# Linear attention twice, gated: loading the first x tile in halves, and one denominator pass per query block

## The chip, the cores and the metric

The kernel runs on one core of one Trainium2 chip. Its time is the device time of one execution in microseconds; lower is better. The time before is the median of 4 runs.

## The reference

Two linear attention blocks A and B read the same x (2048 x 640, bf16) with weights of their own; a gate mixes them.

```python
# x: [1, 2048, 640]; H = 32 heads of 20
qkv = (x @ wqkv).reshape(B, S, 3, H, Dh) ...        # q, k, v
phi = lambda t: jnp.where(t > 0, t + 1, jnp.exp(t)) + 1e-6
pq, pk = phi(q), phi(k)
kv  = jnp.einsum("bhsd,bhse->bhde", pk, v)
z   = jnp.einsum("bhsd->bhd", pk)
num = jnp.einsum("bhqd,bhde->bhqe", pq, kv)
den = jnp.einsum("bhqd,bhd->bhq", pq, z)[..., None] + 1e-6
block = (num / den) ... @ wo
# with g = sigmoid(sum(x * gate_w)):
out = g * A_block + (1 - g) * B_block
```

## The kernel before, in words

**Names.** XN is x by rows (16 tiles of 128 rows), XT its transpose. WK, WQ, WV, WO are the weights of A and B; a weight's "chunk" c is 128 of its 640 rows. PK and PQ are the features phi(k) and phi(q); they share one buffer, FEA for A and FEB for B, so the profile calls both FEA or FEB. ps is PSUM, 8 banks of 512 float columns.

**Stages.** First, keys: x tiles 0 to 3 are loaded by rows and transposed on TensorE (`transpose_x`, L480), and DVE copies the transposes from PSUM to XT (L488); tiles 4 to 15 come transposed by DMA. `k_part` multiplies a tile by WK in 5 chunks; `phi_k` makes the features with one ACT exponential (L506) and two DVE instructions (L510, L515). Second, `g_unit` multiplies the key features by x, which gives the sums from which `m_unit` (a product with WV and a mask into MB on DVE, L607) and `wp_unit` (a product of MB with WO, copied to WS) build one matrix WP per attention block; WP goes through DRAM (`wrows`) by `wp_rows`. The sums of the key features end up in ZBD. Third, queries: `q_unit` makes 512 columns of query features for one of 5 feature groups: 5 matmuls of 512 columns, an exponential on ACT into one of 6 EK slots (L699), and two DVE instructions (L703, L708) that end in PQ. Ten units (5 of A, 5 of B) make a block of 512 rows; there are 4 blocks. Then `dens` multiplies PQ by ZBD, 4 narrow column groups side by side (two for A, two for B), and `scale_q` adds eps (L743), takes the reciprocal (L749), sends it through DRAM to be spread over heads (`factor`, RX), and multiplies PQ by it in place (L767). Last, `final` multiplies PQ of a tile of 128 rows by WP, for A and for B, and mixes both with the gate (ACT L815, DVE L821) before the output DMA.

**Order.** All operations are listed in the program with the keys they read and write. A planner (`_Sched.schedule`) fixes at build time the order of each engine, with estimated durations: it gives each engine the operation that can start first, and among those within 20 ns the one that comes first in the program. PSUM banks, EK slots and the like are handed out in the same walk. On the chip every engine then runs its list in order and waits on semaphores. The operations of the first key tiles are chained (`after=at[0]`), so TensorE does them in program order:

```python
warm(7)
transpose_x(0)
warm(1)
transpose_x(1)
first("A", (0, 0), (0, 1))          # (tile, chunk)
warm(1)
first("A", (1, 0), (1, 1))
first("A", (0, 2), (1, 2), (0, 3), (1, 3))
transpose_x(2)
```

`warm` is a matmul of 512 columns on constants. DMAs are issued from SP's and from ACT's queue; all matmuls but the transposes are recorded at L395, all DMAs at L384.

Of the kernel before, what the change touches and what calls it, by code (L numbers as in the profile page):

```python
# [19 lines left out]
D = 640  # L20
# [4 lines left out]
NC = 5  # L25
EPS = 1e-6
HALF = 320
XW = 672
PE_GHZ = 2.4

# [276 lines left out]
def _dve_ns(n, rate=1):  # L307
    return n / (0.96 * rate) + 68.0
# [6 lines left out]
def bass_gated_mix__linear_attn_block__linear_attn_block__prompt_kernel(nc, A_x, A_wqkv, A_wo, B_x, B_wqkv, B_wo, gate_w, out):  # L315
# [6 lines left out]
    with ExitStack() as es:  # L322
# [89 lines left out]
            ),  # L412
            400, writes=[("ID",)], name="id1",
        )
        for X in XS:
            sch.op("POOL", lambda e, X=X: e.memset(WO[X][:, 5, :], 0.0), 500, writes=[("WO5", X)], name="woz" + X)
        sch.op("POOL", lambda e: e.memset(MB[:, 5, :], 0.0), 200, writes=[("M", 5)], name="mz")
        def load_x(eng, t):
            dma(eng, "xn%d" % t, XN[:, t, 0:D], xin[128 * t : 128 * t + 128, :], writes=[("XN", t)], us=0.25)

        def load_wk(eng, c):
            dma(eng, "wkA%d" % c, WK["A"][:, c, :], weights("A", D, c, c + 1)[:, 0, :], writes=[("WK", "A", c)], us=0.25)

        load_wk("ACT", 0)
        load_x("SP", 0)
        load_wk("ACT", 1)
        load_x("SP", 1)
        load_wk("ACT", 2)
        load_wk("SP", 3)
        load_wk("ACT", 4)  # L430
        load_x("SP", 2)
        load_x("ACT", 3)
        for c0, c1 in ((0, 1), (1, 3), (3, 5)):
            dma(
                "SP", "wkB%d" % c0, WK["B"][:, c0:c1, :], weights("B", D, c0, c1), writes=[("WK", "B", c) for c in range(c0, c1)],
# [38 lines left out]
        def transpose_x(t):  # L474
            tt = _Tile(1)

            def fn(pe):
                ins = None
                for c in range(NC):
                    ins = pe.transpose(PSB[:, tt.banks[0], 128 * c : 128 * c + 128], XN[:, t, 128 * c : 128 * c + 128], IDN[:, :])  # L480
                return ins

            at[0] = sch.op(
                "PE", fn, 5 * 112, reads=[("XN", t), ("ID",)], writes=[(tt,)], name="xpose%d" % t, lat=190, after=at[0]
            )
            sch.op(
                "DVE",
                lambda e: e.tensor_copy(  # L488
                    XT[:, :, 128 * t : 128 * t + 128], PSB[:, tt.banks[0], 0:D].rearrange("p (c f) -> p c f", f=128)
                ),  # L490
                _dve_ns(D), reads=[(tt,)], writes=[("XT", t)], name="xev%d" % t,
            )

        ring = {"ek": _Ring(NEK), "dn": _Ring(2), "rx": _Ring(2), "os": _Ring(NOS), "ts": _Ring(NTS)}

# [26 lines left out]
        def k_part(X, t, tile, cs, chain=False):  # L522
            xc = slice(128 * t, 128 * t + 128)
            order = [(h, c) for h in (0, 1) for c in cs] if len(cs) == NC else [(h, c) for c in cs for h in (0, 1)]

            def steps():
                return [
                    (PS[:, tile.banks[h], 0:HALF], XT[:, c, xc], WK[X][:, c, HALF * h : HALF * h + HALF], c == 0, c == NC - 1, None)
                    for h, c in order
                ]  # L530

            o = mms(
                "k%s%d_%d" % (X, t, cs[0]), steps, [("XT", t)] + [("WK", X, c) for c in cs], [(tile,)], len(cs) * (D + 12),
                after=at[0] if chain else None,
            )
            if chain:
                at[0] = o
# [81 lines left out]

        def wp_unit(X, q):  # L620
            tile = _Tile(2)
            n = 120

            def steps():
                return [
                    (PS[0:n, tile.banks[h], 0:HALF], MB[0:n, q, 0:n], WO[X][0:n, q, HALF * h : HALF * h + HALF], True, True, None)
                    for h in (0, 1)
                ]

            mms("wp%s%d" % (X, q), steps, [("M", q), ("WO", X), ("WO5", X)], [(tile,)], D + 60)  # L630
            dst = WS[0:n, q, :].rearrange("p (h f) -> p h f", f=HALF)

            def src():
                return PS[0:n, tile.banks[0] : tile.banks[1] + 1, 0:HALF]

            name = "wpe%s%d" % (X, q)
            if X == "A" and q % 2 == 0:
                sch.op("DVE", lambda e: e.tensor_copy(dst, src()), _dve_ns(D), reads=[(tile,)], writes=[("WS", q)], name=name)
            else:
                sch.op("ACT", lambda e: e.activation(dst, src(), ACT.Copy), _act_ns(D), reads=[(tile,)], writes=[("WS", q)], name=name)  # L640
# [39 lines left out]
        def q_unit(X, b, k):  # L680
            tile = _Tile(1)
            es = _Tile(1, ring["ek"])

            def ek():
                return EK[:, es.slot, 0:512]

            dst = PQ[X][:, k, 512 * b : 512 * b + 512]
            span = range(S * k + 512 * b, S * k + 512 * b + 512)
            over = [("F", X, "k", t) for t in range(span[0] // D, span[-1] // D + 1)]

            def steps():
                return [
                    (PS[:, tile.banks[0], :], WQ[X][:, c, k : D : NC], XT[:, c, 512 * b : 512 * b + 512], c == 0, c == NC - 1, None)
                    for c in range(NC)
                ]

            mms("q%s%d%d" % (X, b, k), steps, [("XT", t) for t in range(4 * b, 4 * b + 4)] + [("WQ", X)], [(tile,)], NC * 518, after=gone[X])
            sch.op(
                "ACT", lambda e: e.activation(ek(), PS[:, tile.banks[0], :], ACT.Exp), _act_ns(512), reads=[(tile,)],  # L699
                writes=[(es,)], name="eq%s%d%d" % (X, b, k),  # L700
            )
            sch.op(
                "DVE", lambda e: e.tensor_scalar(ek(), ek(), 1.0, EPS, op0=ALU.min, op1=ALU.add), _dve_ns(512, 4),  # L703
                reads=[(es,)], writes=[(es,)], name="tq%s%d%d" % (X, b, k),
            )
            sch.op(
                "DVE",
                lambda e: e.scalar_tensor_tensor(  # L708
                    out=dst, in0=PS[:, tile.banks[0], :], scalar=0.0, in1=ek(), op0=ALU.max, op1=ALU.add
                ),  # L710
                _dve_ns(512), reads=[(tile,), (es,)], writes=[("PQ", X, k, b)] + over, name="sq%s%d%d" % (X, b, k),
            )

        def dens(b0):

            dtile = _Tile(1)

            def den():
                r = []
                for k in range(NC):  # L720
                    for x, X in enumerate(XS):
                        q = PQ[X][:, k, 512 * b0 : 512 * b0 + 1024].rearrange("p (b h f) -> p b h f", b=2, h=2)
                        for h in (0, 1):
                            g = 2 * x + h
                            r.append((
                                PS[32 * g : 32 * g + 32, dtile.banks[0], :].rearrange("p (b f) -> p b f", b=2), ZBD[X][:, k, :],
                                q[:, :, h, :], k == 0, k == NC - 1, (0, 32 * g),
                            ))
                return r

            mms(
                "den%d" % b0, den, [("ZBD", X) for X in XS] + [("PQ", X, k, b) for X in XS for k in range(NC) for b in (b0, b0 + 1)],
                [(dtile,)], 5 * 540,
            )
            return dtile

        def scale_q(b, dtile, pieces):

            ds = _Tile(1, ring["dn"])
            lo = 256 * (b % 2)  # L740
            sch.op(
                "DVE",
                lambda e: e.tensor_scalar(DN[:, ds.slot, :], PS[:, dtile.banks[0], lo : lo + 256], EPS, None, op0=ALU.add), _dve_ns(256),  # L743
                reads=[(dtile,)], writes=[(ds,)], name="dn%d" % b,
            )

# [135 lines left out]
            wp_unit("A", q)  # L882
        wp_rows("A")
        zbd("B")
        def queries(b):
            for X in XS:
                for k in range(NC):
                    q_unit(X, b, k)
                    if b == 1 and X == "A":
                        wp_unit("B", k)  # L890

        def finals(b):
            for t in range(4 * b, 4 * b + 4):
                if t < NT - 1:
                    final(t)
                else:
                    final(t, ((0, 320), (320, 480), (480, D)), {320: 0, D: 320})

        queries(0)
        m_unit("B", 0)  # L900
        m_unit("B", 1)
        queries(1)
        wp_unit("B", 5)
        wp_rows("B")
        d01 = dens(0)
        scale_q(0, d01, 2)
        queries(2)
        queries(3)
        scale_q(1, d01, 2)
        d23 = dens(2)  # L910
        finals(0)
        scale_q(2, d23, 2)
        finals(1)
        scale_q(3, d23, 4)
        finals(2)
        finals(3)

        sch.schedule()
        sch.plan()
# [31 lines left out]
```

## Time and profile before

| | |
|---|---|
| median of 4 runs | 193.91 us (193.54 to 195.27) |
| profiled execution | 195.42 us, span 193.6 us, 1.82 us around it |
| PE busy | 187.7 us, 97% of the span |
| DVE busy | 129.6 us, 67% |
| ACT busy | 73.6 us, 38% |
| granted TensorE clock | 1.00 in the whole span |
| keys | PE from 4.9 us |
| queries | PE from 97.8 to 146.0 us |
| finals | PE from 146.0 to 191.0 us |

The span runs from the first to the last instruction of the profiled execution. Busy time is the time in which an engine has an instruction running; idle time counts only where the engine that sets the end is idle. Rows give engine, line of the source, operation, and what is written from what. A matmul row lasts longer than its place in the stream, since matmuls overlap; the distance between the starts of two rows is what one of them costs.

### The profile page before, as it was taken

The numbers are of one execution on the slowest core, as the hardware profiler recorded it, in microseconds if no ns is written. First come the engines' busy times: TensorE is split into PE (matmuls) and PEld (weight loads), VectorE is DVE, ScalarE is ACT, GpSimd is POOL, SyncE is SP. The second block draws the span as 40 slices with busy tenths as digits, with TensorE's granted clock in tenths as the row PEclk, the third lists the DMA queues.
The fourth block names the chain that finished last, engine by engine and source line by source line (L and its number), as shares of the span: only waits on it lengthen the run. The fifth ranks groups of instructions, "written<-read, shape, count | busy, mean of one in ns | idle before, by whom it ended". The sixth has DMA issues, their size and how long they took to land.

```text
span 193.6 us, 3194 instructions
## 1 busy us (share of the span) xinstructions
PE 187.7 (97%) x1318; PEld 133.1 (69%) x1323; DVE 129.6 (67%) x249; ACT 73.6 (38%) x112; POOL 2.7 (1%) x12
## 2 busy tenths in 40 slices
PE   8699999999999999999999999999999999999994
PEld 3477777777788888888865655555556677777773
DVE  1188888888800008995169977899999997943323
ACT  2055455454411111203265477645654223332232
POOL 5000000000000000000000000000000000000000
PEclk9999999999999999999999999999999999999999
DMA  6989799996012311121145402353300135411112
GB/s 179 310 164 204 139 389 253 295 245 172 7 28 40 37 34 34 34 37 34 34 89 133 156 0 64 109 176 115 97 0 3 36 128 153 141 65 40 68 68 68
DMA packets 30609, 21.17 MB, mean 109 GB/s; under 512 B 15492, under 2 KB 30340, under 8 KB 30596
## 3 DMA queue, kind: packets, MB, share of 16 engines
q1 hardware_dynamic: 29876, 20.16, 40.8%
q10 hardware_dynamic: 720, 0.82, 1.3%
q8 instruction: 10, 0.16, 0.4%
q14 instruction: 3, 0.02, 0.0%
HBM read 12.06 MB, written 5.31 MB: 90 GB/s over the span
## 4 chain that ended last, share of the span: by engine, by line
PE 93%; DMA 3%; DVE 1%; ACT 1%; ACTq 0%; issue 0%
PE ps L395 92%; DMA WKA<-in_A_wqkv_dram 3%; DVE MB L607 1%; ACTq L384 0%; DVE FEB L708 0%; ACT EK L699 0%; PE ps L480 0%; ACT TS L815 0%; DVE OL L821 0%; DVE EK L703 0%
## 5 line engine op out<-in xcount | busy, mean ns | idle before, releaser
L506 ACT ACTIVATE EK<-ps 128x640 bf16<-128x640 f32 x32 | 22.4, 703 | 25.0 <-PE ps L395 25.0
L699 ACT ACTIVATE EK<-ps 128x512 bf16<-128x512 f32 x40 | 23.9, 597 | 20.1 <-PE ps L395 19.6
L815 ACT ACTIVATE TS<-ps,GA 128x640 f32<-128x640 f32 (+2 forms) x18 | 13.2, 734 | 31.0 <-PE ps L395 31.0
L395 PE MATMUL ps<-WPB,FEB 128*128 128x320 bf16 (+1 forms) x165 | 24.7, 295 | 0.0
L395 PE MATMUL ps<-WPA,FEA 128*128 128x320 bf16 (+1 forms) x165 | 24.7, 295 | 0.0
L395 PE MATMUL ps<-WKA,XT 128*128 128x320 bf16 x160 | 23.1, 299 | 1.6 <-DMA WKA<-in_A_wqkv_dram 1.6
L395 PE MATMUL ps<-XT,WQA 128*128 128x512 bf16 x96 | 22.6, 379 | 0.2
L395 PE MATMUL ps<-XN,FEB 128*128 128x320 bf16 (+1 forms) x160 | 22.5, 300 | 0.0
L395 PE MATMUL ps<-WKB,XT 128*128 128x320 bf16 x160 | 22.4, 299 | 0.0
L395 PE MATMUL ps<-XT,WQB 128*128 128x512 bf16 x99 | 22.2, 379 | 0.1
L395 PE MATMUL ps<-XN,FEA 128*128 128x320 bf16 (+1 forms) x160 | 22.0, 300 | 0.0
L821 DVE SCALAR_TENSOR_TENSOR OS<-ps,GA,TS 128x640 bf16<-128x640 f32 x15 | 13.0, 874 | 12.8 <-PE ps L395 11.4
L557 ACT ACTIVATE GS<-ps 128x640 bf16<-128x640 f32 x10 | 7.0, 703 | 37.1 <-PE ps L395 37.1
L395 PEld LDWEIGHTS ps<-XN,FEA 128*128 128x128 bf16 x160 | 18.8, 117 | 3.0
L395 PEld LDWEIGHTS ps<-WKA,XT 128*128 128x128 bf16 x160 | 15.4, 98 | 7.9 <-DMA WKA<-in_A_wqkv_dram 1.9
L395 PEld LDWEIGHTS ps<-XN,FEB 128*128 128x128 bf16 x160 | 18.7, 118 | 2.9
L395 PEld LDWEIGHTS ps<-WPA,FEA 128*128 128x128 bf16 x165 | 15.9, 98 | 6.1
L395 PEld LDWEIGHTS ps<-WPB,FEB 128*128 128x128 bf16 x165 | 15.8, 98 | 6.2 <-issue 0.4
L395 PEld LDWEIGHTS ps<-WKB,XT 128*128 128x128 bf16 x160 | 15.7, 98 | 6.1
L395 PEld LDWEIGHTS ps<-XT,WQB 128*128 128x128 bf16 x100 | 11.7, 117 | 9.7
L395 PEld LDWEIGHTS ps<-XT,WQA 128*128 128x128 bf16 x100 | 11.6, 118 | 8.8 <-issue 0.4
L661 DVE SCALAR_TENSOR_TENSOR GP<-XN,GWB 128x640 bf16<-128x640 bf16 x16 | 13.3, 833 | 4.1 <-PE ps L395 3.6
(52 smaller groups left out, 151.2 us busy)
## 6 DMA issues: line engine op xcount, KB each, us to landing
out_dram<-OS SPq DMA_DIRECT2D x15, 160.0 KB, 1.8
XN<-in_A_x_dram SPq DMA_DIRECT2D x3, 640.0 KB, 8.4
factor<-RC SPq DMA_DIRECT2D x4, 256.0 KB, 2.6
RX<-factor SPq DMA_DIRECT2D x4, 256.0 KB, 2.7
WVA<-in_A_wqkv_dram SPq DMA_DIRECT2D x1, 800.0 KB, 12.4
WQA<-in_A_wqkv_dram SPq DMA_DIRECT2D x1, 800.0 KB, 15.5
WVB<-in_B_wqkv_dram SPq DMA_DIRECT2D x1, 800.0 KB, 16.9
WQB<-in_B_wqkv_dram SPq DMA_DIRECT2D x1, 800.0 KB, 16.5
```

Source lines behind the costliest of these rows:

```text
L395: ins = pe.matmul(o, l, r, start=a, stop=z, tile_position=tp, skip_group_check=True)
L506: "ACT", lambda e: e.activation(ek2(), pair(tile, HALF), ACT.Exp),
L557: "ACT", lambda e: e.activation(GS[:, k, :].rearrange("p (h f) -> p h f", f=HALF), pair(tile, HALF), ACT.Copy),
L607: return e.tensor_tensor(out=MB[0:n, qq[0] : qq[-1] + 1, 0:n].rearrange("p q (i k) -> p q k i", k=NC), in0=PS[0:n, tile.banks[0], at : at ...
L661: lambda e, t=t: e.scalar_tensor_tensor(out=GP[:, :], in0=XN[:, t, 0:D], scalar=1.0, in1=GWB[:, :], op0=ALU.mult, op1=ALU.mult, accum_out= ...
L699: "ACT", lambda e: e.activation(ek(), PS[:, tile.banks[0], :], ACT.Exp), _act_ns(512), reads=[(tile,)],
L815: "ACT", lambda e, acc=acc, t_ap=t_ap: e.activation(t_ap(), acc(), ACT.Copy, scale=GA[:, 0, t : t + 1]),
L821: lambda e, acc=acc, t_ap=t_ap, o_ap=o_ap: e.scalar_tensor_tensor(out=o_ap(), in0=acc(), scalar=GA[:, 1, t : t + 1], in1=t_ap(), op0=ALU.m ...
```

## The change

- The first x tile is loaded as two column halves, one on SP's queue and one on ACT's, both ahead of the WK chunks, and the chunks and the next x tiles are dealt anew over the two queues.
- The DVE copies of the transposes of tiles 0 and 1 go in two pieces (chunks 0 and 1, then 2 to 4), and a key product waits for the piece with its chunk alone.
- Three memsets on POOL are gone; the product for WP's last group of 40 rows uses 40 rows instead of 120 rows with zeros.
- Denominators: one pass per query block with 256 columns a matmul, 4 passes, where there was one per two blocks with 512 columns, 2 passes.
- The order at the end: each block's factor follows its queries, and the finals of block b - 2 follow the queries of block b.

```diff
--- before.py
+++ after.py
@@ -25,6 +25,7 @@
 NC = 5
 EPS = 1e-6
 HALF = 320
+AHEAD = 2
 XW = 672
 PE_GHZ = 2.4
 
@@ -412,24 +413,25 @@
             ),
             400, writes=[("ID",)], name="id1",
         )
-        for X in XS:
-            sch.op("POOL", lambda e, X=X: e.memset(WO[X][:, 5, :], 0.0), 500, writes=[("WO5", X)], name="woz" + X)
-        sch.op("POOL", lambda e: e.memset(MB[:, 5, :], 0.0), 200, writes=[("M", 5)], name="mz")
         def load_x(eng, t):
             dma(eng, "xn%d" % t, XN[:, t, 0:D], xin[128 * t : 128 * t + 128, :], writes=[("XN", t)], us=0.25)
 
         def load_wk(eng, c):
             dma(eng, "wkA%d" % c, WK["A"][:, c, :], weights("A", D, c, c + 1)[:, 0, :], writes=[("WK", "A", c)], us=0.25)
 
+        for eng, h in (("SP", 0), ("ACT", 1)):
+            dma(
+                eng, "xn0_%d" % h, XN[:, 0, HALF * h : HALF * h + HALF], xin[0:128, HALF * h : HALF * h + HALF],
+                writes=[("XN0", h)], us=0.15,
+            )
         load_wk("ACT", 0)
-        load_x("SP", 0)
         load_wk("ACT", 1)
         load_x("SP", 1)
-        load_wk("ACT", 2)
-        load_wk("SP", 3)
-        load_wk("ACT", 4)
-        load_x("SP", 2)
-        load_x("ACT", 3)
+        load_wk("SP", 2)
+        load_wk("ACT", 3)
+        load_wk("SP", 4)
+        load_x("ACT", 2)
+        load_x("SP", 3)
         for c0, c1 in ((0, 1), (1, 3), (3, 5)):
             dma(
                 "SP", "wkB%d" % c0, WK["B"][:, c0:c1, :], weights("B", D, c0, c1), writes=[("WK", "B", c) for c in range(c0, c1)],
@@ -481,15 +483,17 @@
                 return ins
 
             at[0] = sch.op(
-                "PE", fn, 5 * 112, reads=[("XN", t), ("ID",)], writes=[(tt,)], name="xpose%d" % t, lat=190, after=at[0]
-            )
-            sch.op(
-                "DVE",
-                lambda e: e.tensor_copy(
-                    XT[:, :, 128 * t : 128 * t + 128], PSB[:, tt.banks[0], 0:D].rearrange("p (c f) -> p c f", f=128)
-                ),
-                _dve_ns(D), reads=[(tt,)], writes=[("XT", t)], name="xev%d" % t,
-            )
+                "PE", fn, 5 * 112, reads=[("XN", t), ("ID",)] + [("XN0", h) for h in (0, 1)][: 2 - 2 * min(t, 1)], writes=[(tt,)], name="xpose%d" % t, lat=190, after=at[0]
+            )
+            for c0, c1 in ((0, 2), (2, NC)) if t < 2 else ((0, NC),):
+                sch.op(
+                    "DVE",
+                    lambda e, c0=c0, c1=c1: e.tensor_copy(
+                        XT[:, c0:c1, 128 * t : 128 * t + 128],
+                        PSB[:, tt.banks[0], 128 * c0 : 128 * c1].rearrange("p (c f) -> p c f", f=128),
+                    ),
+                    _dve_ns(128 * (c1 - c0)), reads=[(tt,)], writes=[("XTC", t, c) for c in range(c0, c1)], name="xev%d" % t,
+                )
 
         ring = {"ek": _Ring(NEK), "dn": _Ring(2), "rx": _Ring(2), "os": _Ring(NOS), "ts": _Ring(NTS)}
 
@@ -530,7 +534,7 @@
                 ]
 
             o = mms(
-                "k%s%d_%d" % (X, t, cs[0]), steps, [("XT", t)] + [("WK", X, c) for c in cs], [(tile,)], len(cs) * (D + 12),
+                "k%s%d_%d" % (X, t, cs[0]), steps, ([("XTC", t, c) for c in cs] if t < 4 else [("XT", t)]) + [("WK", X, c) for c in cs], [(tile,)], len(cs) * (D + 12),
                 after=at[0] if chain else None,
             )
             if chain:
@@ -619,7 +623,7 @@
 
         def wp_unit(X, q):
             tile = _Tile(2)
-            n = 120
+            n = 120 if q < 5 else 40
 
             def steps():
                 return [
@@ -694,7 +698,7 @@
                     for c in range(NC)
                 ]
 
-            mms("q%s%d%d" % (X, b, k), steps, [("XT", t) for t in range(4 * b, 4 * b + 4)] + [("WQ", X)], [(tile,)], NC * 518, after=gone[X])
+            mms("q%s%d%d" % (X, b, k), steps, ([("XT", t) for t in range(4 * b, 4 * b + 4)] if b else [("XTC", t, c) for t in range(4) for c in range(NC)]) + [("WQ", X)], [(tile,)], NC * 518, after=gone[X])
             sch.op(
                 "ACT", lambda e: e.activation(ek(), PS[:, tile.banks[0], :], ACT.Exp), _act_ns(512), reads=[(tile,)],
                 writes=[(es,)], name="eq%s%d%d" % (X, b, k),
@@ -711,36 +715,28 @@
                 _dve_ns(512), reads=[(tile,), (es,)], writes=[("PQ", X, k, b)] + over, name="sq%s%d%d" % (X, b, k),
             )
 
-        def dens(b0):
-
+        def scale_q(b, pieces):
+
+            ds = _Tile(1, ring["dn"])
             dtile = _Tile(1)
 
             def den():
                 r = []
                 for k in range(NC):
                     for x, X in enumerate(XS):
-                        q = PQ[X][:, k, 512 * b0 : 512 * b0 + 1024].rearrange("p (b h f) -> p b h f", b=2, h=2)
                         for h in (0, 1):
                             g = 2 * x + h
+                            s0 = 512 * b + 256 * h
                             r.append((
-                                PS[32 * g : 32 * g + 32, dtile.banks[0], :].rearrange("p (b f) -> p b f", b=2), ZBD[X][:, k, :],
-                                q[:, :, h, :], k == 0, k == NC - 1, (0, 32 * g),
+                                PS[32 * g : 32 * g + 32, dtile.banks[0], 0:256], ZBD[X][:, k, :], PQ[X][:, k, s0 : s0 + 256],
+                                k == 0, k == NC - 1, (0, 32 * g),
                             ))
                 return r
 
-            mms(
-                "den%d" % b0, den, [("ZBD", X) for X in XS] + [("PQ", X, k, b) for X in XS for k in range(NC) for b in (b0, b0 + 1)],
-                [(dtile,)], 5 * 540,
-            )
-            return dtile
-
-        def scale_q(b, dtile, pieces):
-
-            ds = _Tile(1, ring["dn"])
-            lo = 256 * (b % 2)
+            mms("den%d" % b, den, [("ZBD", X) for X in XS] + [("PQ", X, k, b) for X in XS for k in range(NC)], [(dtile,)], 5 * 270)
             sch.op(
                 "DVE",
-                lambda e: e.tensor_scalar(DN[:, ds.slot, :], PS[:, dtile.banks[0], lo : lo + 256], EPS, None, op0=ALU.add), _dve_ns(256),
+                lambda e: e.tensor_scalar(DN[:, ds.slot, :], PS[:, dtile.banks[0], 0:256], EPS, None, op0=ALU.add), _dve_ns(256),
                 reads=[(dtile,)], writes=[(ds,)], name="dn%d" % b,
             )
 
@@ -882,38 +878,25 @@
             wp_unit("A", q)
         wp_rows("A")
         zbd("B")
-        def queries(b):
+        for b in range(NB):
             for X in XS:
                 for k in range(NC):
                     q_unit(X, b, k)
                     if b == 1 and X == "A":
                         wp_unit("B", k)
-
-        def finals(b):
-            for t in range(4 * b, 4 * b + 4):
-                if t < NT - 1:
+            if b == 1:
+                wp_unit("B", 5)
+                wp_rows("B")
+            scale_q(b, 2 if b < NB - 1 else 4)
+            if b == 0:
+                m_unit("B", 0)
+                m_unit("B", 1)
+            if b >= AHEAD:
+                for t in range(4 * (b - AHEAD), 4 * (b - AHEAD) + 4):
                     final(t)
-                else:
-                    final(t, ((0, 320), (320, 480), (480, D)), {320: 0, D: 320})
-
-        queries(0)
-        m_unit("B", 0)
-        m_unit("B", 1)
-        queries(1)
-        wp_unit("B", 5)
-        wp_rows("B")
-        d01 = dens(0)
-        scale_q(0, d01, 2)
-        queries(2)
-        queries(3)
-        scale_q(1, d01, 2)
-        d23 = dens(2)
-        finals(0)
-        scale_q(2, d23, 2)
-        finals(1)
-        scale_q(3, d23, 4)
-        finals(2)
-        finals(3)
+        for t in range(4 * (NB - AHEAD), 4 * NB - 1):
+            final(t)
+        final(4 * NB - 1, ((0, 320), (320, 480), (480, D)), {320: 0, D: 320})
 
         sch.schedule()
         sch.plan()
```

## The prediction

> **What bounds the kernel now.** I read the page first (busy shares and the chain that ended last), then the list of who waited for whom, then the PE, DVE and SP timelines around the places the diff touches.
>
> ```profile
> PE 187.7 (97%) x1318; PEld 133.1 (69%) x1323; DVE 129.6 (67%) x249; ACT 73.6 (38%) x112; POOL 2.7 (1%) x12
> ...
> PE 93%; DMA 3%; DVE 1%; ACT 1%; ACTq 0%; issue 0%
> ```
>
> PE is the bound: the chain is 93% PE, and its only other large piece is a DMA at the start. So an edit counts only if it changes PE's column work, or one of PE's few waits. These are the waits (waiting engine, releaser, total us, times, longest):
>
> ```profile
> PE ps L395 <- DMA WKA<-in_A_wqkv_dram: 1.6, 1, 1.6
> PE ps L395 <- PEq L936: 0.8, 1, 0.8
> PE ps L395 <- DVE MB L607: 0.6, 1, 0.6
> ```
>
> The 0.8 is the program's start. What is left to gain is 1.6 us at the front and 0.6 us in the middle. Both in the PE timeline (start, length, what):
>
> ```profile
> 4.90 0.72 PE L395 MATMUL ps<-WKA,XT 128*128 128x320 bf16 x4
> 5.46 0.38 PE L395 MATMUL ps<-const-bfloat16-1.0 128*128 128x512 bf16 x1
> 5.67 0.71 PE L395 MATMUL ps<-WKA,XT 128*128 128x320 bf16 x4
> 7.98 1.26 PE L395 MATMUL ps<-WKA,XT 128*128 128x320 bf16 x8 [1.60 <-DMA WKA<-in_A_wqkv_dram]
> ...
> 111.73 0.48 PE L395 MATMUL ps<-WOB,MB 120*120 120x320 bf16 x2 [0.61 <-DVE MB L607]
> ```
>
> From 7.98 on, PE runs on without a DMA wait; whatever moves that restart moves the end.
>
> **Part 1, the first loads.** The wait at 7.98 is for wk chunk 2, third on ACT's queue (issued at 1.66, 6.3 us to land). On each queue the first two transfers land early and the third late:
>
> ```profile
> WKA<-in_A_wqkv_dram ACTq DMA_DIRECT2D x1, 160.0 KB, 6.3
> WKA<-in_A_wqkv_dram SPq DMA_DIRECT2D x1, 160.0 KB, 5.5
> ```
>
> ACT: chunk 0 at 0.73+3.1 = 3.8, then chunk 2 at 7.9, chunk 4 at about 2.1+6.6 = 8.7. SP: x0 at 3.6, x1 at about 4.4, chunk 3 at 7.2, x2 at 2.13+6.0 = 8.1. After the change the queues hold: ACT x0 (half), wk 0, wk 1, wk 3, x2; SP x0 (half), x1, wk 2, wk 4, x3. So wk 1, which PE wants before chunk 2, moves into the third place on ACT. Each queue carries 80 KB less ahead of its third transfer; 160 KB at the 347 to 364 GB/s that the windows from 6 to 9 us show is 0.45 us. By place, wk 1 lands at 7.93 - 0.45 = 7.5, wk 2 at 6.7, wk 3 at 8.3. PE does chunk 0 of tile 0, waits until 7.5, and then still has chunk 1 of tile 0, a warm-up matmul, and chunks 0 and 1 of tile 1: 6 matmuls at 0.136 (ten take 1.36 in the finals) + 0.216 = 1.03. Chunk 2 starts at 8.5, against 7.98: +0.5. Chunk 3 is wanted at 9.1, x2 at 9.6 (lands 9.2 by place), so no second wait.
>
> If the third transfers land with no gap, PE runs on by itself: tile 1's chunks 0 and 1 ended at 5.67+0.54 = 6.2 before, and the split copy and half load may take up to 0.3 off. That is 7.98 - 5.9 = -2.0. If the third place costs the full 7.93, it is +1.0. The profiled execution took 195.42 (span 193.6 and 1.82 around it), 1.5 above the median of the runs shown, 193.91, so in others the wait may be shorter on both sides. I take +0.3, nearer to the places seen; ends -2.0 and +1.0.
>
> A rule that speaks against the halves: the Trainium skill, "DMA: Bandwidth & Descriptors", "Rules for kernel authors", says that transfers issued from several engines share the same DMA engines, and that splitting one over two queues gains no bandwidth. By it alone the halves would land when the whole tile did, a gain of 0. In the trace x0 and wk 0, issued together at 0.73 on two queues, landed at 3.6 and 3.8, which fits; the sum does not need it.
>
> **Part 2, the copies in two pieces.** A whole copy of 640 takes 0.49; the first chunk could start some 0.2 earlier. It stands ahead of the wait for wk 1, which hides it: 0 (with that cover gone, -0.2, inside the -2.0).
>
> **Part 3, what the queues and POOL do besides.** SP issues one transfer more, 0.43 each, so wkB, the transposed x and all behind come 0.43 later. Cover: the last wkB lands near 3.6+7.5 = 11.1 and is read after 12.76; the first transposed block lands at 4.07+10.3 = 14.4 and is read near 18.2. Uncovered it would cost 0.43. ACT issues five as before. POOL's three memsets that go (0.63, 0.63, 0.20) feed nothing before the first mask, past 80 us; the 40-row product of group 5 streams the same 320 columns. All 0.
>
> **Part 4, the denominators.** Two passes of 20 x 512 columns become four of 20 x 256. Four column groups run side by side:
>
> ```profile
> 123.14 2.32 PE L395 MATMUL ps<-XT,WQA 128*128 128x512 bf16 x10
> 125.39 0.39 PE L395 MATMUL ps<-FEA,ZBDA 128*32 128x512 bf16 x2
> ...
> 126.27 0.38 PE L395 MATMUL ps<-FEA,ZBDA 128*32 128x512 bf16 x2
> ...
> 126.59 3.43 PE L395 MATMUL ps<-XT,WQA 128*128 128x512 bf16 x14
> ```
>
> Ten query matmuls at 0.216 (25 take 5.39, 129.86 to 135.25) from 123.14 end at 125.30; the next starts at 126.59, so a pass holds PE for 1.29. Its five steps are 0.216 apart, 1.08; the rest, 0.21, is an edge. With half the columns a pass is 0.54 + 0.21 = 0.75. Four of them are 3.0, against 2.58: +0.42. Below: if the edge halves too, 0. Above: the narrow matmuls of the B product run 30 in 1.67 (108.42 to 110.09), 0.056 each; at that pace 80 need 4.5, with edges 5.3: +2.7. The four groups start within 0.02 of each other, far under 0.056, so I take +0.42.
>
> **Part 5, the order of the second half.** Block 0's denominator now comes right after its queries. The planner gives an engine the operation that can start first, and of those within 20 ns the earliest in program order; worked through by hand from 108 us that gives PE: the B product to 110.09, one query unit to 111.17, the first short pass to 111.9, and only then the WOB product that had waited until 111.73 for the mask. The stall of 0.61 goes: -0.61 (its other end is 0, if the mask came later still; DVE started it at 110.18, right after the block's last query instruction, and would again).
>
> DVE is the cost. Behind the mask (2.0) now come DN 0.33 and RC 1.67, then four multiplies of 0.74 when the factor has made its DMA round trip, 5.4 after RC (129.26 to 134.65 before). When it is behind, DVE takes 0.80 per query unit (138.29 to 139.89 for two); PE takes 1.08. Counted through, DVE: 110.27 + 2.0 + 2.0 + ten units 8.0 + multiplies 2.9, and some 1.5 in which it waits for PE (the WOB products stretch PE's unit to 1.36), is 126.7 at the end of block 1; 2.0 + 8.0 + 2.9 more is 139.6 at the end of block 2. PE: 111.9 + six WOB products of 0.27 + nine units 9.7 = 123.2, then 10.8 + 0.75 = 134.8. DVE lags by 3.5 and 4.8. Before, at the end of block 3, it lagged by 149.5 - 146.2 = 3.3 and PE did not wait. Six EK slots hold 6 x 1.08 = 6.5. So no stall: 0; the end above is rival C's. Finals of block 0, 10.9 us on PE against 3.5 on DVE, then give the time back. They need WP of B, which landed at 125.85+4.3 = 130.2 and is wanted at 134.8. At the end, block 3's factor is ready near 167 and its finals start at 179, so the tail (last matmul to last write) stays as it is: 0.
>
> **Sum.** +0.3 + 0.42 - 0.61 = +0.1. Against the profiled 195.42 that is 195.5; on the median 193.91 it is 194.0.
>
> **Rivals.** *A, the forecast:* small terms of both signs, 194.0; its own range 192.9 to 195.6. *B, the front clears:* the third transfers land without a gap, because each queue carries less ahead of them. For it: the first two of each queue landed 0.8 apart, so a third could be there near 5. Against: the new order still puts two wk chunks third on both queues, as before, and PE now needs both of these. -2.0 + 0.42 - 0.61 = -2.2: 191.7. *C, DVE becomes the bound* where block 2 ends and block 0's finals begin. If DVE runs query units unpaired, 0.97 each (0.287 + 0.685) in place of 0.80, 20 units add 3.4 to the lag of 4.8: 8.2. PE then waits for banks from the point where the lag passes what they hold: 6.5 for query units, but 4 x 1.08 = 4.3 if the finals, which need two banks side by side, find none. The wait is 1.7 by the one and 3.9 by the other, 2.8 between: 196.8. For it: the mask and two factor computations fall into a stage where DVE was 68 to 91% busy (windows 112 to 124), and the finals come at once behind. Against: DVE paired its instructions by itself when it fell behind, and a final's tile on ACT's side is free within 1 us. *D, denominators at the narrow pace:* +2.7 in place of +0.42: 196.3. Against: the 0.02 spacing.
>
> **How the numbers follow.** A 0.58, B 0.16, C 0.18, D 0.08. Some 1% (1.9 us) is what a measurement of this kernel tells from no change. Faster by more: B, 0.16. Within: A, 0.58. Slower by more: C and D, 0.26. The range reaches into B, to 191.9, and past D to most of C, 196.8.
>
> **What would show it.** Front: the first wait for WKA now names chunk 1, and the 8 matmuls of chunks 2 and 3 start near 8.5; a start before 7 is B. Middle: no wait on MB; four ZBDA passes of 0.75 each. DVE: PE shows no wait on L708 between 115 and 146; one of over 1 us is C. The end after the last matmul is unchanged. Wrong would be any PE wait that none of these names.

## The result, and the profile after

The change makes the kernel slightly slower: median 194.98 us over 54 runs against 194.53 over 78 runs of the kernel before, ratio 1.0028 with a 95% interval of 1.0016 to 1.0039. That is +0.54 us (0.31 to 0.76). The prediction said 194.0 from a smaller set of runs before (193.91), that is +0.1, within 1% likeliest.

The profiled execution of the change says the opposite: 194.50 us with a span of 192.9, where that of before took 195.42 and 193.6. The page of the change, busy shares and chain:

```profile
PE 188.3 (98%) x1357; PEld 133.5 (69%) x1363; DVE 128.7 (67%) x251; ACT 73.5 (38%) x112; POOL 1.2 (1%) x9
...
PE 94%; DMA 3%; ACTq 1%; issue 0%; ACT 0%; DVE 0%
```

PE is still the bound. These are the waits of PE in the change (waiting engine, releaser, total us, times, longest); the 0.8 is the program's start:

```profile
PE ps L396 <- PEq L919: 0.8, 1, 0.8
...
PE ps L482 <- DMA XN<-in_A_x_dram: 0.3, 1, 0.3
...
PE ps L396 <- DMA WKA<-in_A_wqkv_dram: 0.2, 1, 0.2
PE ps L396 <- issue: 0.2, 1, 0.2
```

The wait on the mask MB is gone, and no wait on DVE's L712 took its place. The row with "issue" stands ahead of a query matmul at 96.93, where the record of the unit's first matmul is missing (the trace has 24 of 25); it is no wait. The 0.3 for XN, at tile 2's rows, is one that the prediction had not expected ("no second wait"). The front in the PE timeline of the change:

```profile
4.72 0.45 PE L396 MATMUL ps<-WKA,XT 128*128 128x320 bf16 x2
5.34 0.45 PE L396 MATMUL ps<-WKA,XT 128*128 128x320 bf16 x2 [0.18 <-DMA WKA<-in_A_wqkv_dram]
5.63 0.38 PE L396 MATMUL ps<-const-bfloat16-1.0 128*128 128x512 bf16 x1
5.84 1.79 PE L396 MATMUL ps<-WKA,XT 128*128 128x320 bf16 x12
7.93 0.45 PE L482 MATMUL ps<-IDN,XN 128*128 128x128 bf16 x5 [0.29 <-DMA XN<-in_A_x_dram]
```

The first wait for WKA is now at chunk 1 of tile 0, as predicted, but it lasts 0.18 here, and chunk 2 follows near 6.4 and not at 8.5 (near 8.1 in e1 and 7.1 in e9, which have the same loads). A single execution can't price this front: the start of the first WKB product, which closes it, lies between 11.26 and 12.89 in nine profiled executions with the loads of before (those with the longer warm-up left out), and at 11.76, 12.02 and 13.04 in three with the loads of the change. So the second half is read from the traces, from the first product of the key sums (`g`) to the end of the last matmul, where executions repeat to 0.02; the front is read from times alone. In the change this stretch runs from 49.79 to 190.03, 140.24; before, from 50.93 to 191.00, 140.07. The second half lost 0.17 where the prediction had -0.19.

The places in it, in the PE timeline of the change:

```profile
109.18 1.03 PE L396 MATMUL ps<-XT,WQA 128*128 128x512 bf16 x4
110.13 0.29 PE L396 MATMUL ps<-FEA,ZBDA 128*32 128x256 bf16 x2
...
110.58 0.28 PE L396 MATMUL ps<-FEA,ZBDA 128*32 128x256 bf16 x2
...
110.83 0.48 PE L396 MATMUL ps<-WOB,MB 120*120 120x320 bf16 x2
...
122.06 0.45 PE L396 MATMUL ps<-WOB,MB 40*40 40x320 bf16 x2
122.44 4.51 PE L396 MATMUL ps<-XT,WQA 128*128 128x512 bf16 x19
126.88 0.29 PE L396 MATMUL ps<-FEA,ZBDA 128*32 128x256 bf16 x2
```

The first short pass stands where PE had waited for the mask, and the product follows it without a wait. The five steps of a pass are 0.11 apart. The 40-row product holds PE for 0.38 until the next query matmul; on 120 rows, before, it was 0.28 until the one at 123.14:

```profile
122.86 0.44 PE L395 MATMUL ps<-WOB,MB 120*120 120x320 bf16 x2
```

### The profile page after: what moved, and what is told of

Read it like the earlier page. It is cut to its first block, busy times and chain, and to the rows that moved or that the text cites. A ratio compares the mean times of both kernels' runs of the same rounds, so it can differ in the third digit from the quotient of the medians.

```text
span 192.9 us, 3268 instructions
## 1 busy us (share of the span) xinstructions
PE 188.3 (98%) x1357; PEld 133.5 (69%) x1363; DVE 128.7 (67%) x251; ACT 73.5 (38%) x112; POOL 1.2 (1%) x9
## 4 chain that ended last, share of the span: by engine, by line
PE 94%; DMA 3%; ACTq 1%; issue 0%; ACT 0%; DVE 0%
PE ps L396 94%; DMA XN<-in_A_x_dram 3%; ACTq L385 1%; PE ps L482 0%; ACT TS L811 0%; DVE OL L817 0%
```

## The experiments

Ratios are to the kernel before, timed on the same chip, where its median was 194.33 (e1 to e4), 194.40 (e5 to e9) and 194.42 (e13). They are not quotients of the medians: for e9 the medians differ by -0.13, and the ratio is 1.0009. Differences "by time" are worked out from the ratios.

**Front and second half apart.** e1 puts the change's loads and split copies on the kernel before; e2 is the change without them.

```diff
+ for eng, h in (("SP", 0), ("ACT", 1)):      # e1: before + these loads
+     dma(eng, "xn0_%d" % h, ...)             #     and the copies in two pieces
...
- for eng, h in (("SP", 0), ("ACT", 1)):      # e2: the change - these loads
```

> The kernel before with the front of the change alone: x tile 0 in halves, the loads dealt as in the change, the copies of tiles 0 and 1 in two pieces. Theory 1 (the front costs: wk chunk 1 in the third place of its queue lands late): about 0.5 us slower than before, as in the prediction, 195.0. Theory 2 (the front gains what the one profiled execution shows, 1.1 us, and the second half loses it again): 0.5 to 1.1 us faster than before, near 193.5.

> The change without its front: four denominator passes, the new order, the 40-row product, with loads and copies as before. Theory 1: the terms of the second half cancel (+0.5 for the passes, -0.6 for the mask wait, +0.2 for the step from finals back to queries): within 0.2 us of before, 194.5. Theory 2: 0.5 to 1.5 us slower than before, 195.0 to 196.0.

Measured: e1 194.52, ratio 1.0015 (0.9996 to 1.0034); e2 194.82, ratio 1.0028 (1.0010 to 1.0046). The front comes to +0.3 us (-0.1 to +0.7), which can't be told from 0, the second half to +0.5 (0.2 to 0.9). Theory 2's gain at the front is excluded; but theory 1's "terms cancel" fell too, since e2's interval leaves out 0. The traces show 0.18 of it: from `g` to the last matmul e1 has 140.07, as before, and e2 has 140.25, as the change.

Another part stands outside the span, where no trace looks: a run's time less the span recorded for it. With the old second half the time outside is 1.89 or less in all 132 runs that have a span; with the new one (the change, e2, e4, e9, e13) it is 2.0 to 3.1 in 27 of 96, which adds 0.2 to 0.3 on average in the change, e2, e9 and e13. Why is not shown. Another difference there costs nothing: with the new loads the time outside is mostly 1.5 and not 1.8, but the span goes on for 2.86 after the last matmul and not for 2.59.

**The first loads out of the way.** Both kernels with a longer warm-up.

```diff
-        warm(7)
+        warm(35)
```

> The kernel before with 28 more warm-up matmuls of 0.216 us, 6.05 us, ahead of the first transpose, so that all first loads have landed. If the wait of 1.6 us for wk chunk 2 stands in most executions, 4.4 us slower than before (it is absorbed): 199.0. If it stands in few, 6.0 slower: 200.6.

> The changed kernel with the same 28 more warm-up matmuls. Theory 1: with the first loads out of the way only the second half and the split copies are left, so it is 0 to 0.3 us faster than the kernel before with the same matmuls. Theory 2: 0.5 us or more slower than that kernel, since the second half is what costs.

Measured: e3 200.13, ratio 1.0294 (1.0268 to 1.0320), +5.7 us: nearer to 6.0 than to 4.4. By itself that says little, since in the profiled execution of e3 the 28 matmuls move the first transpose by 6.78 (3.71 to 10.49) and not by 6.05. The traces of the other kernels say it directly: chunk 2 landed at 7.93 in the profiled execution of before, and at 5.32 to 7.80 in the nine others with the same loads. PE waited for it 1.60 there, 0.65 in e2, 0.40 in e8, 0.33 in e11, and not at all in e5, e6, e10, e12 and e13. The 1.6 us wait is the longest of nine.

e4 200.66, ratio 1.0315 (1.0290 to 1.0341): 0.5 us slower than e3 by the medians, with intervals that overlap. That is a miss for theory 1 by its number, and it doesn't settle the matter: the two profiled executions differ in the warm-up itself. The weight loads of the warm-up matmuls, in e3 and in e4:

```profile
4.57 0.15 PEld L395 LDWEIGHTS ps<-const-bfloat16-1.0 128*128 128x128 bf16 x1 [0.28 <-issue]
5.00 5.16 PEld L395 LDWEIGHTS ps<-const-bfloat16-1.0 128*128 128x128 bf16 x24 [0.28 <-issue]
```

```profile
5.84 0.15 PEld L396 LDWEIGHTS ps<-const-bfloat16-1.0 128*128 128x128 bf16 x1 [0.28 <-issue]
6.27 0.15 PEld L396 LDWEIGHTS ps<-const-bfloat16-1.0 128*128 128x128 bf16 x1 [0.28 <-issue]
6.63 4.26 PEld L396 LDWEIGHTS ps<-const-bfloat16-1.0 128*128 128x128 bf16 x20 [0.22 <-issue]
```

One matmul every 0.43 until about 5.0 in e3 and until 6.6 in e4, then one every 0.215. The same list of matmuls ends 0.74 later in e4. With 0.20 less at the copies (below) and 0.19 more from `g` to the last matmul, that is the 0.73 by which e4's last matmul ends later.

**The 40-row product alone.** A row of the change that the prediction had put at nothing; it is in e2 and not in e1.

```diff
-            n = 120
+            n = 120 if q < 5 else 40        # e8: on the kernel before; e9 undoes it in the change
```

> The kernel before with one edit: the product for the last group of WP's rows uses 40 rows instead of 120 (A and B, two matmuls each). Theory 3 (a product on 40 rows drains the array at its edges, as the denominator passes do; the traces of the change show 0.23 more around A's and 0.19 more around B's): 0.4 us slower than before. The prediction's reading (the same 320 columns, so nothing): within 0.2 us of before.

> The changed kernel with that product on 120 rows again, the padding set to zero on POOL as before. Theory 3: 0.4 us faster than the change, so within 0.3 us of the kernel before. The prediction's reading: as the change, 0.5 us slower than before.

Measured: e8 194.89, ratio 1.0034 (1.0012 to 1.0057), +0.66 us (0.23 to 1.1). e9 194.27, ratio 1.0009 (0.9992 to 1.0026), against 1.0028 for the change. In the traces `g` to the last matmul is 140.52 in e8, +0.45 on before; in e9 it is 139.78, -0.46 on the change. Four matmuls with fewer rows cost about as much as the whole change. The prediction's "same columns, so nothing" is excluded by e8.

**Which side of the product it is.** Three kernels, read by their traces, with other sizes for the product of the last group.

```diff
-  MB[0:n, q, 0:n], WO[X][0:n, q, ...]         # before: n = 120
+  MB[0:kr, q, 0:n], WO[X][0:kr, q, ...]       # last group: e10 kr, n = 80, 80; e11 120, 40; e12 40, 120
```

> The kernel before with the last group's product on 80 rows in and out. If the drain of 0.2 us at the 40-row product comes with any product smaller than the 120 of its neighbours, the PE timeline shows it here too (0.38 from the product to the next query matmul). If it comes when the product no longer needs more than half of the array's 128 rows or columns, there is none: 0.28, as with 120.

> The kernel before with the last group's product on 120 rows in, 40 rows out (a narrow weight load). If the output side makes the drain, 0.2 us at A's and at B's product in the PE timeline; if the input side does, none.

> The kernel before with the last group's product on 40 rows in, 120 rows out. If the input side makes the drain, 0.2 us at A's and at B's product in the PE timeline; if the output side does, none.

The product of B and the query matmul behind it in the PE timelines of e8, e10, e11 and e12, in this order (start, length; the form is rows in * rows out):

```profile
122.64 0.45 PE L395 MATMUL ps<-WOB,MB 40*40 40x320 bf16 x2
123.01 1.27 PE L395 MATMUL ps<-XT,WQA 128*128 128x512 bf16 x5
```

```profile
122.31 0.44 PE L395 MATMUL ps<-WOB,MB 80*80 80x320 bf16 x2
122.58 1.67 PE L395 MATMUL ps<-XT,WQA 128*128 128x512 bf16 x7
```

```profile
122.33 0.45 PE L395 MATMUL ps<-WOB,MB 120*40 120x320 bf16 x2
122.71 1.49 PE L395 MATMUL ps<-XT,WQA 128*128 128x512 bf16 x6
```

```profile
122.25 0.48 PE L395 MATMUL ps<-WOB,MB 40*120 40x320 bf16 x2
122.66 1.71 PE L395 MATMUL ps<-XT,WQA 128*128 128x512 bf16 x7
```

From the product to the next matmul: 0.37, 0.27, 0.38, 0.41. With 80 rows there is no edge, with 40 on either side alone there is. `g` to the last matmul says the same: 140.06 with 80, 140.52 and 140.59 with 40 on one side, against 140.07 before. Where the time goes shows in PE's weight loads, in e8 and then in e10:

```profile
96.90 0.11 PEld L395 LDWEIGHTS ps<-WOA,MB 40*40 40x40 bf16 x2 [0.23 <-issue]
97.27 2.31 PEld L395 LDWEIGHTS ps<-XT,WQA 128*128 128x128 bf16 x12 [0.26 <-issue]
```

```profile
96.39 0.53 PEld L395 LDWEIGHTS ps<-WOA,MB 120*120 120x120 bf16 x4
96.94 2.63 PEld L395 LDWEIGHTS ps<-XT,WQA 128*128 128x128 bf16 x13
```

In e8 the load of the 40-row weights waits 0.23 and starts at 96.90, together with its matmul, and the load behind the product waits 0.26: weights are not loaded ahead across the step in either direction. In e10 the load of the 80-row weights starts at 96.67, 0.13 ahead of its matmul. The Trainium skill, "TensorEngine Tiling (Array Packing)", "Tiling Modes", says that changing the tiling mode drains the engine, and lists tiles of 128, 64 and 32 rows or columns. 40 rows or columns in a 64 tile and 80 in a 128 tile would fit these rows; the traces here don't show the mode itself. The denominator passes, on 32 columns, look alike: ahead of a pass in the change the weight loads wait 0.26 to 0.40.

**The second half without that product.**

> The change's second half on the kernel before (four denominator passes, the new order), with the loads, the copies and the 120-row product as before. By the trace of the kernel with 120 rows and the change's front, 139.78 from the first sum product to the last matmul against 140.07 before: 0.3 us faster than before, 194.1. If it is as slow as the second half with 40 rows (0.5 us slower than before), the product is not what costs there.

Its edit is e2 with n = 120 and the padding's memsets again. Measured: 194.29, ratio 0.9995 (0.9976 to 1.0015), -0.1 us (-0.5 to +0.3). In the trace `g` to the last matmul is 139.78, the expected -0.29. The second half's slowness in e2 is gone. The gain of 0.3 is in the trace and in the spans of the 12 runs (-0.35 on the mean of before, -0.6 to -0.1); in the times it is lost, since 7 of the 12 lie at 2.0 to 2.9 outside the span.

**The split copies alone.**

```diff
-  e.tensor_copy(XT[:, :, ...], ...)                     # one copy of 5 chunks
+  for c0, c1 in ((0, 2), (2, NC)) if t < 2 else ((0, NC),): ...
```

> The kernel before with the copies of tiles 0 and 1 in two pieces and nothing else; x tile 0 whole, loads dealt as before. The wait for wk chunk 2 hides the earlier first chunk: within 0.2 us of before. If instead the copies, not the loads, set the start in most executions: 0.2 to 0.3 us faster.

Measured: 194.22, ratio 0.9995 (0.9980 to 1.0010): nothing that can be told from 0, as predicted for this part. With the loads out of the way the pieces do show: between the second transposes and the first key product PE stands for 0.26 in e3, where the weight load's row names the copy, and for 0.06 in e4. So what the front costs, if anything, comes from the loads.

**The mask wait alone, and a version better than both.**

```diff
-                    if b == 1 and X == "A":
-                        wp_unit("B", k)
+                    if b == 1 and X == "A" and k:
+                        wp_unit("B", k - 1)
+                if b == 1 and X == "A":
+                    wp_unit("B", 4)
```

> The kernel before with one edit of the order: each product of MB with WO of B comes one query unit later in the program, so that PE has a unit to do while DVE makes the mask. If the PE wait of 0.6 us on the mask is on the path, as the prediction has it, 0.6 us faster than before: 193.9. If the wait only moves (to the matrix WP of B or to DVE), within 0.2 us of before.

Measured: 193.49, ratio 0.9954 (0.9940 to 0.9969), -0.9 us (-1.2 to -0.6), faster than both kernels. PE timeline of e6:

```profile
106.78 1.59 PE L395 MATMUL ps<-GTB,WVB 128*128 128x120 bf16 x30
108.22 2.33 PE L395 MATMUL ps<-XT,WQA 128*128 128x512 bf16 x10
110.39 0.44 PE L395 MATMUL ps<-WOB,MB 120*120 120x320 bf16 x2
```

Two query units run where one did, and the product starts without a wait. `g` to the last matmul is 139.24, -0.83. The wait was worth more than its row said. The 30 matmuls of the B product hold PE for 1.44 here (106.78 to 108.22); before, they began at 108.42, and one unit of 1.08 behind them puts the next start at 110.94, where the product came at 111.73: 0.79. The row of 0.61 counts idle time only from the modelled end of the last matmul.

## Why the prediction was right, and which term was not

The measured 194.98 lies inside the range and within 1%, the likeliest case. The sum had +0.1 and the runs +0.54 on their own median of before; by its terms:

| Step | predicted | measured |
|---|---|---|
| first loads and copies | +0.3 (-2.0 to +1.0) | +0.3 (-0.1 to +0.7), e1 by time |
| four short passes for two long | +0.42 | +0.48 by trace |
| the mask wait goes | -0.61 | -0.79 by trace |
| 40-row product | 0 | +0.46 by trace, +0.66 by time (e8) |
| DVE's lag | 0 | 0, no PE wait |
| time outside the span | not in the sum | +0.2 to +0.3 on average, in no trace |

The passes took 0.78, 0.75, 0.75 and 0.75 from start to start, 3.05 in all against 2 x 1.29, and 0.01 more is lost at the matmuls behind them: the edge of 0.21 a pass was read rightly, and rival D (the narrow pace) is out. The step that failed is in Part 3, where the 40-row product "streams the same 320 columns" and was put at 0. An edge like the 0.21 that Part 4 had measured at the denominators comes with it as well, 0.23 a product, and Part 3 did not ask whether fewer rows bring one. The errors of the mask term (-0.18), the passes (+0.06) and the product (+0.46) sum to 0.34, nearly all of the 0.36 between the predicted second half, -0.19, and the traced one, +0.17.

At the front, the mechanism predicted (chunk 1 waits first) is in all three traces of the new loads, with waits of 0.18, 1.31 and 0.32; its price was about right by the times, but that was luck. It took the landing places of one execution for fixed, and that execution was the latest of ten. With the new loads chunk 1, for which the sum had 7.5, landed at 5.30, 5.98, 6.03 and 7.05 (the change, e4, e9, e1). The halves of x tile 0 did land earlier than the whole tile, which Part 1 doubted: at 2.94 to 3.27 in these four, against 3.60 to 4.06 in the ten with the old loads, with 160 KB issued at 0.73 and not 320. PE gained little by it: behind the 7 warm-up matmuls the first transpose starts at 3.71 with the halves and at 3.71 to 4.10 with the whole tile. Rival B (the front clears) is what the profiled execution of the change happens to show, and not what the times show.

Rival C did not come. DVE ended block 1's last unit at 125.75 with PE done at 121.97, a lag of 3.8 (predicted 3.5); block 2's at 136.21 against 134.05, 2.2 (predicted 4.8), because the multiplies by block 1's factor came after the block's last unit (from 136.13) and not before it.

What stays open: whether the front costs anything at all (e1's interval reaches 0), how its loads and the slow start of PE share in it, and what makes the time outside the span longer in some executions of the new second half.

## What to carry to other kernels

When a kernel is bound by TensorE, count the steps between full and small matmuls, not only the columns: a matmul trimmed to 40 rows among full ones cost more here than the zeros that it saved. Fill a wait of PE by moving one ready unit ahead of it, and price the wait from start to start rather than from its idle row. Take no price for the first microseconds from one execution: read them from many times, and the rest from a stretch of the trace that repeats.

## What was not expected of the hardware

- A matmul on 40 rows or 40 columns between larger ones adds about 0.1 on each side, 0.45 for two such products (e8, e11, e12: 0.45 to 0.52); one on 80 adds nothing (e10).
- In the first microseconds a 512-column matmul takes 0.43, later 0.215, with the change at 5.0 in one execution and 6.6 in another, while the page's row of the granted clock shows full speed throughout. The Trainium skill, "TensorE: Matmul & The Clock Gate", Part 1, describes a half-speed state at the start that ends after some 3.4 us of activity, at a moment that varies from run to run; the pace agrees, and the slow part was longer here, from 0.77 on some 4.2 in e3 and 5.9 in e4.
